# A four-layer kernel of window attention and a 2-D Fourier filter: rows of the filter kept on chip for two groups, and nine smaller moves of work between queues and engines

## The chip, the cores and the metric

The kernel runs on one core of one Trainium2 chip. A core has five engines with instruction streams of their own: TensorE (PE in the profile; matmuls, with weight loads shown as PEld), VectorE (DVE), ScalarE (ACT), GpSimd (POOL) and SyncE (SP, which only issues DMAs here). ScalarE and GpSimd issue DMAs too. TensorE's results go to PSUM, eight banks of 128 partitions x 512 fp32; everything else lives in SBUF or in DRAM. The metric is the time of one execution on the device in microseconds, the median of several runs.

## What is computed

The reference applies two kinds of layer in turn, A, B, A, B, to one sequence of S = 2048 rows with D = 576 columns, all in fp32:

```python
def _A_ref(x, wqkv, wo):
    B, S, D = x.shape
    H = 32; Dh = D // H; W = 256
    qkv = (x @ wqkv).reshape(B, S, 3, H, Dh).transpose(2, 0, 3, 1, 4)
    q, k, v = qkv[0], qkv[1], qkv[2]
    scores = jnp.einsum("bhqd,bhkd->bhqk", q, k) * (Dh ** -0.5)
    idx = jnp.arange(S)
    mask = (idx[:, None] - idx[None, :] >= 0) & (idx[:, None] - idx[None, :] < W)
    p = softmax(where(mask, scores, -1e9))
    o = jnp.einsum("bhqk,bhkd->bhqd", p, v)
    return o.transpose(0, 2, 1, 3).reshape(B, S, D) @ wo

def _B_ref(x, w_r, w_i):
    X = jnp.fft.rfft2(x, axes=(-2, -1)) * (w_r + 1j * w_i)
    return jnp.fft.irfft2(X, s=(S, D), axes=(-2, -1))

x = A_x
for _ in range(2):
    x = x + _A_ref(layernorm(x), A_wqkv, A_wo)
    x = x + _B_ref(layernorm(x), B_w_r, B_w_i)
```

## The kernel before

**Order.** Nothing is scheduled by a planner: every engine executes its instructions in the order in which the Python code writes them, and the framework adds a semaphore wait wherever data or a buffer demands it. So a line moved in the code is an instruction moved within its engine's queue, and an instruction that waits holds up all that stands behind it on that engine. A DMA stands in the queue of the engine that issues it. `layer_a` is written for layers 1 and 3 and `layer_b` for layers 2 and 4; the text calls the first A and first B together layer 1 and the second pair layer 2 (`first` is true in the first `layer_b`, `second` in the second `layer_a`).

**Precision.** Many operands are split into a high part (rounded to fp32r, for a faster matmul) and a low part (the rest). `split_w` (L661) does this for the query/key weights: ScalarE copies the high part (`wqh`, L662), and the engine that it is given subtracts the low part (`wql`, L663). `tail_split` and `tails` do the like for the columns left over behind four blocks of 128.

**Layer A.** The sequence is cut into 16 tiles of 128 rows, the heads into 8 groups of 4. The projections `proj` (L1085; nine weight blocks of 128 columns, four stretches of 512 rows each) feed queries and keys through DRAM. Weight blocks are loaded (`w_load`) and split (`w_split`) while the block before them is in use; block 2 is split while block 1 is projected, in the opening of the attention, where GpSimd also has the memsets of L1232 and L1233. For each tile and head, `score_max` (L1142, L1144) makes the scores and takes the masked maximum, `m_rows` sends the maxima back into the query tile (`qs<-mt`), `exps` (L1179, L1180) makes the scores less the maximum and exponentiates them on ScalarE, GpSimd zeroes what lies outside the window (L1182, L1185), and `part` (L1199) sums the weighted values in the one PSUM bank `U`. After each fourth tile ScalarE copies `U` to `us` (L1204). `norm` (L1210) later transposes these sums (`tpo`, L1213), copies them (`ts`, L1215), divides, and stores the heads' outputs to DRAM. `turned` picks the PSUM bank for `tpo`: a bank of the tag "E" or "S" (three of each) early on, and the single bank "pj" at the end.

The loop `bursts` runs this for tiles 0 to 117 in steps of three heads; with each step it takes at most one or two entries (`tasks`) of the list `due`, which holds the pending `norm` and `m_rows` calls, `norm` sorted last. A drain loop (`for t in range(MIX, NX + 2)`, MIX = 118, NX = 128) writes the last ten tiles out. From tile 120 on `behind` prepares the output projection, the class `Out`, beside it: `out.tail` (GpSimd splits the tail of a tile of attention output), `out.turn` (four transposes into `tpa`, L748 to L751, a cast to `oroom`, L753, by the engine given, a subtraction on VectorE, L757), and loads.

**Output projection and the first filter stage.** `unit` makes 128 rows of the output projection (`ops`, L773) and adds the residual; `ahead(u + 2)` turns the tile two further on (`tpo5p`, `tpo6p` are the first PSUM bank of tiles 5 and 6 there, "q" the second); `sums` and `stats` make the normalization. In the second layer `sums` is two squarings on ScalarE, and `norm` there adds `fy`, a scaling on ScalarE and a subtraction on VectorE. The layernorm of layer B and the first transform are fused to this, one tile n2 of 16 after the other. `f3` (`pz`, L295) is the transform along the rows within a tile, and `f4` (L302 to L341) makes its even and odd halves `ye` (128 x 2 x 290): tile by tile ScalarE copies one half (`half`), VectorE adds and subtracts. In the second layer tiles 12 to 14 instead have their subtraction done by GpSimd from a copy of both halves.

**From the first to the second filter stage.** The second stage works on 16 groups g, and group g needs rows 8g to 8g+7 of all 16 tiles. So `f4` stores each tile whole to DRAM (`yd[0]`, L332), and the second stage reads two groups (a pair) back with one 580 KB load (L470). For the first groups this trip would come last, so tiles 0 to 10 are read back early, in place (L341), and from tile FD = 11 on the rows of these groups are sent from `ye` straight into the pair's tile (L327, `ofree<-ye`, 18 KB each). In the first layer this is done for one pair (groups 0, 1), in the second for two (groups 0 to 3). In the second layer tile 13's stores are issued by GpSimd and tile 14's by ScalarE, whose list `send` is called within tile 15's `f4`, behind its copy; the others go by SyncE. 34 matmuls without use (`warm`, L347) keep TensorE running meanwhile.

**The second filter stage.** `pipe(16, ...)` runs per group: `g0` (loads of the pairs), `gw` (weights not yet there, L202, 580 KB for two groups; the first NW pairs are prefetched during the first stage by `pre`), `g1m` (`p`, L482, the transform down the columns, and the products with the filter on VectorE and GpSimd), `g2` (`pq`, L503, back down the columns, and the halves `ze`, stored whole to `yd[1]` (L540)). `ze` has NY buffers, shared with `ye`, and some of the four `eos`. Groups' rows for the first `near` = 3 tiles of the third stage go straight into their tiles `yis` (L510, `ofree<-ze`) from group FG = 11 on, blocks of earlier groups are read back at groups 10 and 13 (L531). Residuals of two tiles at a time are loaded by `ld` into the pair tiles (`xs`), at groups 11 and 13. 36 more `warm` matmuls end this stage in layer 2.

**The third filter stage.** Per tile n2: `ly` reads the tile (for n2 >= 3), `i1` (`pi`, L566) transforms within the tile and adds the residual, `i2` transposes, `i3` (`po`, L257) makes the output rows. In the first layer the second layer A's opening is fused to it.

## Time and profile before

| | |
|---|---|
| runs | 1384.25, 1384.37, 1386.03 us; median 1384.37 us |
| profiled execution | 1387.98 us, of which the span is 1386.2 us |
| TensorE busy | 1344.4 us (97%), mean granted clock 0.993 |
| VectorE busy | 893.2 us (64%) |
| ScalarE busy | 784.9 us (57%) |
| GpSimd busy | 644.5 us (46%) |
| DMA | 259.12 MB, mean 187 GB/s |

The span begins with the first and ends with the last recorded event of one profiled execution; the time of that execution has 1.8 us around it. Busy time is the sum of an engine's own instructions, without waits and without issuing DMAs. "PE p L482 <- DMA ofree<-ye: 7.3, 1, 7.3" in a list of waits says that the matmuls of line 482 that write `p` waited for a DMA from `ye` into `ofree` (the big tile which holds the pair tiles), 7.3 us in all, once, at the longest 7.3. A row of a timeline gives the start in us, the duration, the engine, line, operation, output<-inputs with shapes, and in brackets the idle time of the engine before it and what ended it; `SPq` and `ACTq` are the queues of SyncE and ScalarE at their DMA issues. A row of the stretches has, behind the window: the span of the core that falls in it; the busy time of PE, PEld, and then of DVE, ACT and POOL, each with its number of instructions; the granted TensorE clock as a share of full speed; the share of time in which the DMA engines were busy; and GB/s.

### The profile page before, as it was taken

How to read it: one execution, taken by the hardware profiler on the slowest of the kernel's cores; microseconds unless marked ns; L12 is line 12 of the kernel's file. 1: busy time of each engine (PE TensorE's matmuls, PEld its weight loads, DVE VectorE, ACT ScalarE, POOL GpSimd, SP SyncE). 2: the span in 40 equal slices, each digit the busy share in tenths (PEclk: the TensorE clock that was granted, in tenths of full speed). 3: DMA queues.
4: the chain of work that ended last, by engine and by line, in shares of the span. 5: the costliest groups of instructions: out<-in, count | busy, mean ns of one | idle time of the engine just before them, and what ended most of it. 6: DMA issues, size and time to landing. Idle time of an engine off the chain costs nothing.

```text
span 1386.2 us, 33596 instructions
## 1 busy us (share of the span) xinstructions
PE 1344.4 (97%) x11356; PEld 1001.6 (72%) x11356; DVE 893.2 (64%) x3046; ACT 784.9 (57%) x1978; POOL 644.5 (46%) x1152
## 2 busy tenths in 40 slices
PE   9999999999999999999999999999999999997998
PEld 8985656666665699975999965566666655996588
DVE  5417777777778266666663157777778774574855
ACT  5622767777778544542455316677777778463223
POOL 2257545555546533476221394455455458111821
PEclk9999999999999999999999999999999999999999
DMA  6756655655446447678763467565554564597874
GB/s 200 209 165 187 192 181 163 187 170 165 149 143 183 123 146 250 221 233 272 262 217 73 127 189 219 158 175 166 159 157 138 160 173 134 154 380 225 275 235 160
DMA packets 202480, 259.12 MB, mean 187 GB/s; under 512 B 104589, under 2 KB 109965, under 8 KB 201797
## 3 DMA queue, kind: packets, MB, share of 16 engines
q1 hardware_dynamic: 191573, 235.70, 56.2%
q10 hardware_dynamic: 7856, 15.33, 3.2%
q0 software_dynamic: 2880, 5.93, 1.7%
q8 instruction: 92, 1.51, 0.5%
q14 instruction: 79, 0.65, 0.1%
HBM read 155.98 MB, written 101.01 MB: 185 GB/s over the span
## 4 chain that ended last, share of the span: by engine, by line
PE 81%; DMA 5%; ACT 4%; POOL 3%; DVE 3%; issue 2%; SPq 1%; ACTq 0%; DVEq 0%; POOLq 0%
PE pj L1085 17%; PE S L1142 12%; PE U L1199 11%; PE vps L978 8%; PE ops L773 7%; PE E L1179 5%; PE po L257 4%; PE pf L257 2%; PE p L482 2%; PE pi L566 2%; PE pq L503 2%; PE tpo L1213 2%; ACT P L1180 2%; DMA qs<-mt 2%; PE pz L295 2%
## 5 line engine op out<-in xcount | busy, mean ns | idle before, releaser
L1144 DVE CUSTOM_DVE_ANT_0 jk<-S,mask 128x384 bf16<-128x384 f32 (+2 forms) x1024 | 491.0, 528 | 120.1 <-PE E L1179 58.8
L1180 ACT ACTIVATE P<-E 128x384 f32<-128x384 f32 (+2 forms) x1024 | 409.8, 477 | 129.8 <-PE E L1179 101.6
L1182 POOL TENSOR_SCALAR_AFFINE_SELECT P<-P 128x512 f32<-128x512 f32 x256 | 162.5, 635 | 288.1 <-ACT P L1180 264.2
L1142 PE MATMUL S<-ks,qs 63*128 63x384 f32 (+2 forms) x1024 | 269.7, 373 | 0.6 <-DVE m L1144 0.4
L1179 PE MATMUL E<-qs,ks 64*128 64x384 f32 (+2 forms) x1024 | 224.0, 373 | 7.3 <-DMA qs<-mt 5.0
L1142 PEld LDWEIGHTS S<-ks,qs 63*128 63x128 f32 x1024 | 141.0, 186 | 105.3 <-DVE m L1144 72.8
L1199 PE MATMUL U<-P,vq 128*19 128x128 f32 (+1 forms) x3840 | 188.4, 329 | 0.9 <-ACT us L1204 0.9
L1085 PE MATMUL pj<-xh,wqh 128*128 128x512 f32 x360 | 157.6, 438 | 1.3 <-DVE sg L1100 0.8
L1199 PEld LDWEIGHTS U<-P,vq 128*19 128x19 f32 x3840 | 96.0, 99 | 78.0 <-issue 23.0
L1185 POOL TENSOR_SCALAR_AFFINE_SELECT P<-P 128x512 f32<-128x512 f32 x224 | 142.1, 634 | 0.0
L1179 PEld LDWEIGHTS E<-qs,ks 64*128 64x128 f32 x1024 | 114.7, 186 | 23.0 <-ACT P L1180 10.4
L1085 PE MATMUL pj<-xh,wql 128*128 128x512 f32 x360 | 125.0, 420 | 2.7 <-POOL wql L663 2.7
L1085 PE MATMUL pj<-xl,wqh 128*128 128x512 f32 x288 | 123.1, 427 | 0.0
L773 PE MATMUL ops<-oroom 128*128 128x290 f32 (+1 forms) x812 | 115.3, 298 | 0.2
L773 PEld LDWEIGHTS ops<-oroom 128*128 128x128 f32 x812 | 110.3, 189 | 0.7 <-DVE ofree L796 0.7
L1085 PEld LDWEIGHTS pj<-xh,wqh 128*128 128x128 f32 x360 | 68.4, 190 | 32.4 <-issue 11.0
L1100 DVE TENSOR_TENSOR sg<-pj,sg 128x512 fp32r<-128x512 f32 x72 | 49.5, 687 | 56.1 <-ACT sg L1097 56.1
L1144 DVE DVE_READ_ACCUMULATOR2_ANT m<- 128x1 f32 x1024 | 84.8, 83 | 0.0
L1097 ACT CAST sg<-pj 128x512 fp32r<-128x512 f32 x72 | 42.2, 586 | 73.3 <-PE pj L1085 58.0
L1085 PEld LDWEIGHTS pj<-xh,wql 128*128 128x128 f32 x360 | 64.4, 189 | 23.5 <-issue 10.7
L978 PE MATMUL vps<-wvh,xh 128*128 128x288 f32 x320 | 71.5, 305 | 0.0
L1085 PEld LDWEIGHTS pj<-xl,wqh 128*128 128x128 f32 x288 | 54.9, 190 | 18.2 <-issue 11.4
(596 smaller groups left out, 2260.7 us busy)
## 6 DMA issues: line engine op xcount, KB each, us to landing
qk_d<-sg SPq DMA_DIRECT2D x56, 512.0 KB
qs<-qk_d SPq DMA_DIRECT2D x384, 72.0 KB
ks<-qk_d SPq DMA_DIRECT2D x348, 72.0 KB
v_d<-vt SPq DMA_DIRECT2D x32, 304.0 KB
vq<-v_d SPq DMA_DIRECT2D x16, 608.0 KB
wt<-in_w SPq DMA_DIRECT2D x16, 580.0 KB
ofree<-x SPq DMA_DIRECT2D x16, 580.0 KB
x<-ofree SPq DMA_DIRECT2D x32, 290.0 KB
```

The source lines that it names most:

```text
L257: T.matmul(ps[:, c, 0:NF], tail[r] if si == 4 else hl_(si), dcs[b // 2][r, b % 2], start=mi == si == 0, stop=si == 4)
L773: self.nc.tensor.matmul(self.ps[u][n][:, 0:self.n], x, self.w[p][:, (2 * wk + n) * self.n:(2 * wk + n + 1) * self.n], start=first and i == ...
L978: T.matmul(ps[:, n, 0:288], xT(xk, c), w[:, wk, n * 288:(n + 1) * 288], start=i == 0, stop=i == len(ks) - 1)
L1085: T.matmul(box["ps"].rearrange("r (n p) -> r n p", n=NT) if second else box["ps"], w[:, wk], x, start=s == 0, stop=s == len(ks) - 1)
L1100: V.tensor_sub(rest[:, 1], by, rest[:, 0].bitcast(F32))
L1142: T.matmul(ps[:, 0:N], q[b:b + 63, pair, i * 128:i * 128 + 128], k[b:b + 63, pair, lo:hi], start=True, stop=True)
L1144: V.tensor_tensor_reduce(out=jk[:, 0:N], in0=ps[:, 0:N], in1=mask[:, 384 - N:384], scale=1.0, scalar=-3e38, op0=ALU.add, op1=ALU.max, accu ...
L1179: T.matmul(ps[:, 0:nq], k[b:b + 64, pair, j * 128:j * 128 + 128], q[b:b + 64, pair, j * 128:j * 128 + nq], start=True, stop=True)
L1180: A.activation(p[:, hl_, 0:nq], ps[:, 0:nq], AF.Exp, scale=SC)
L1182: P.affine_select(out=p[:, :, 0:128], in_=p[:, :, 0:128], pattern=[[0, 4], [1, 128]], compare_op=ALU.is_ge, fill=0.0, base=0, channel_mult ...
L1185: P.affine_select(out=p[:, :, 256:384], in_=p[:, :, 256:384], pattern=[[0, 4], [-1, 128]], compare_op=ALU.is_gt, fill=0.0, base=0, channel ...
L1199: T.matmul(U[32 * h:32 * h + 19, (q0 % 4) * 128:(q0 % 4) * 128 + 128 * (q1 - q0)], vts[n][:, j, h], pt[n, j][:, h, (q0 - j) * 128:(q1 - j) ...
```

## The change

- **Rows (second layer's `f4`).** Rows are sent straight for groups 0 and 1 alone, with one in-place load; `ye` has five buffers. Tile 12 goes by SyncE as before, with two rows less. Tiles 13, 14 and 15 are held and all sent within tile 15's `f4`, behind its two VectorE instructions, in this order: tile 13's two rows (GpSimd), tile 14's first (SyncE) and second (GpSimd), tile 15's two (SyncE), then whole tile 13 (GpSimd), whole 15 (SyncE), whole 14 (GpSimd). GpSimd thus has done all three of its subtractions before it issues any of them, and ScalarE issues none. In the second layer the pair of groups 2 and 3 is read back from DRAM like the others, in two halves.
- **Filter weights.** NW is 5 in both layers: the sixth pair of weights in the second layer is loaded in the second stage.
- **Residual load behind the last stores.** `ld(0)` stays at group 11; `ld(2)` moves from group 13 to the end of group 15, behind the last stores.
- **Rows of groups 13 and 14 for the second tile** go by GpSimd at group 14.
- **Tile 3's load first.** `ly` issues tile 3's load at n2 = 0 and the later ones as before.
- **Tile 2's sums (second layer).** `sums(2)` and `norm(2)` move from ahead of the loop to behind `unit(3)` and `ahead(5)`.
- **Weight 2's low part** is subtracted by VectorE; the other blocks stay with GpSimd.
- **Last sums and transposes.** For the last twelve tiles `us` is copied by VectorE; in the drain `ts` is copied by VectorE, and `tpo` of blocks c > 1 takes a bank of tag "S". The last step of `bursts` takes no tasks, and `due` is sorted once more before the drain.
- **Tails** of tiles 0 to 2 are split one query tile earlier in the drain; tile 3's is split at the same place as before.

```diff
@@ -144,7 +144,7 @@
     yd = [dram.tile([16, 16, 8, 2 * NF], F32, name=f"yd{j}") for j in range(2)]
     OPEN = *range(2, 17, 2), 17
     FD, FG, SH = 11, 11, 192
-    near, NY = 3, 3 if first else 4
+    near, NY = 3, 3 if first else 5
...
@@ -203,7 +203,7 @@
...
-        NW = 5 if first else 6
+        NW = 5
 
         def pre(n2):
 
@@ -310,35 +310,42 @@
             else:
                 both = ip.tile([128, 2, NF], F32, tag="both", name=f"half{n2}", bufs=2)
                 A.copy(both[:, 0], pz[:, 1, 0:NF])
-                if not first and n2 == NT - 1:
-                    hs[n2 - 1]["send"]()
                 V.tensor_add(ye[:, 0], pz[:, 0, 0:NF], both[:, 0])
                 V.tensor_sub(ye[:, 1], pz[:, 0, 0:NF], both[:, 0])
             yef = ye.rearrange("p j f -> p (j f)")
             pre(n2)
-            wide = 1 if first else 2
             if n2 == FD:
-                for k in range(wide):
-                    y_tile(k)
-            eng = nc.sync if n2 < NT - 3 or n2 == NT - 1 else P if first is (n2 == NT - 2) else nc.sync if first else nc.scalar
-
-            def rows(lo, hi):
-                for g in range(lo, hi):
-                    eng.dma_start(ys[g][8 * n2:8 * n2 + 8].rearrange("p c f -> p (c f)"), yef[8 * g:8 * g + 8])
-
-            def send():
-                if n2 >= FD:
-                    rows(0, 2 if n2 == NT - 1 else 2 * wide)
+                y_tile(0)
+
+            def row(eng, g):
+                eng.dma_start(ys[g][8 * n2:8 * n2 + 8].rearrange("p c f -> p (c f)"), yef[8 * g:8 * g + 8])
+
+            def whole(eng):
                 eng.dma_start(yd[0][:, n2], yef)
-                if n2 == NT - 1:
-                    rows(2, 2 * wide)
-            if eng is nc.scalar:
-                h["send"] = send
+
+            if n2 < FD:
+                whole(nc.sync)
+            elif first or n2 < NT - 3:
+                e = P if n2 == NT - 2 else nc.sync
+                for g in range(2):
+                    row(e, g)
+                whole(e)
             else:
-                send()
+                h["rows"] = [lambda e, g=g: row(e, g) for g in range(2)]
+                h["whole"] = whole
+            if not first and n2 == NT - 1:
+                a, b, c = hs[n2 - 2:]
+                a["rows"][0](P)
+                a["rows"][1](P)
+                b["rows"][0](nc.sync)
+                b["rows"][1](P)
+                c["rows"][0](nc.sync)
+                c["rows"][1](nc.sync)
+                a["whole"](P)
+                c["whole"](nc.sync)
+                b["whole"](P)
             if n2 == FD:
-                for k in range(wide):
-                    nc.sync.dma_start(pairs[k].rearrange("p (a f) -> p a f", a=2)[0:8 * FD], yd[0][2 * k:2 * k + 2, 0:FD].rearrange("a n i f -> (n i) a f"))
+                nc.sync.dma_start(pairs[0].rearrange("p (a f) -> p a f", a=2)[0:8 * FD], yd[0][0:2, 0:FD].rearrange("a n i f -> (n i) a f"))
 
         def warm(n):
 
@@ -436,13 +443,15 @@
                 if u > 5:
                     out.load_o(u)
                 out.tail(u)
-            for u in (1, 2):
-                out.sums(u)
-                norm(u)
+            out.sums(1)
+            norm(1)
             for u in range(3, NT - 1):
                 out.load_x(u + 2)
                 out.unit(u, pp)
                 out.ahead(u + 2, pp, False)
+                if u == 3:
+                    out.sums(2)
+                    norm(2)
                 if u + 5 < NT:
                     out.load_o(u + 5)
                     out.tail(u + 5)
@@ -466,7 +475,7 @@
         def g0(g, h):
             if g % 2 == 0 and g not in ys:
                 y = y_tile(g // 2).rearrange("p a c f -> p a (c f)")
-                for a in ((0, 1), (1, 2)) if g == (2 if first else 4) else ((0, 2),):
+                for a in ((0, 1), (1, 2)) if g == 2 else ((0, 2),):
                     nc.sync.dma_start(y[:, a[0]:a[1]], yd[0][g + a[0]:g + a[1]].rearrange("a n i f -> (n i) a f"))
             h["y"] = ys[g]
 
@@ -482,8 +491,8 @@
                     T.matmul(ps[64 * j:64 * j + 64, c, 0:NF], fc[:, g, j, c], h["y"][:, j], start=True, stop=g > 0)
                     if g == 0:
                         T.matmul(ps[64 * j:64 * j + 64, c, 0:NF], fc[:, 16, j, c], h["y"][:, 1 - j], start=False, stop=True)
-            if g in (11, 13):
-                ld(g - 11)
+            if g == 11:
+                ld(0)
             w = wt[g]
             p1 = tws[g % 2]
             p2 = wp.tile([128, 2, NF], F32, tag="tc", name=f"p2_{g}", bufs=3)
@@ -530,11 +539,13 @@
                 for n2 in range(near):
                     nc.sync.dma_start(yis[n2][8 * lo:8 * hi].rearrange("p c f -> p (c f)"), yd[1][n2, lo:hi].rearrange("g i f -> (g i) f"))
             if g == 14:
+                rows(P, 1, 13)
+                rows(P, 1, 14)
                 for k in range(FG, 14):
                     rows(P, 2, k)
             if FG <= g < 15:
-                for n2 in range(2):
-                    rows(P if g == 14 and n2 else nc.sync, n2, g)
+                for n2 in range(1 if g > 12 else 2):
+                    rows(nc.sync, n2, g)
 
             def store():
                 (P if g == 14 else nc.scalar if g < 13 and (g < 8 or g % 2 == 0) else nc.sync).dma_start(yd[1][:, g], yef)
@@ -542,6 +553,8 @@
                 held.append(store)
             else:
                 store()
+            if g == 15:
+                ld(2)
 
         zs, held = {}, []
         pipe(16, [(10, g2), (7, g1m), (2, gw), (0, g0)])
@@ -555,9 +568,9 @@
             next(nxt)
 
         def ly(n2, h):
-            y = h["y"] = yis[n2 % 4]
-            if n2 >= near:
-                nc.sync.dma_start(y.rearrange("p c f -> p (c f)"), yd[1][n2].rearrange("g i f -> (g i) f"))
+            h["y"] = yis[n2 % 4]
+            for k in (near,) if n2 == 0 else (n2,) if n2 > near else ():
+                nc.sync.dma_start(yis[k % 4].rearrange("p c f -> p (c f)"), yd[1][k].rearrange("g i f -> (g i) f"))
 
         def i1(n2, h):
             pi = pp.tile([128, 2, 512], F32, tag="mm", name=f"pi{n2}", bufs=3)
@@ -873,7 +886,7 @@
             h = bp.tile([128, 5, 128], F32R, tag="wqh", name=f"wqh{i}", bufs=2)
             l = bp.tile([128, 5, 128], F32R, tag="wql", name=f"wql{i}", bufs=2)
             wt[i] = (h, l)
-            split_w(nc, raw, h, l, P)
+            split_w(nc, raw, h, l, V if i == 2 else P)
             if i + 2 < 9:
                 w_load(i + 2)
 
@@ -1201,18 +1214,18 @@
                                  start=j == max(e - 1, 0), stop=j == i or (i == e and j == i - 2), skip_group_check=True)
                 if half and i % 4 == 3:
                     us[n, i // 4] = u = wp.tile([128, 512], F32, tag="us", name=f"us{n}_{i}", bufs=1)
-                    A.copy(u, U)
+                    (V.tensor_copy if x >= MIX - 2 else A.copy)(u, U)
 
             def pv(x):
                 part(x, 0)
                 part(x, 1)
 
-            def norm(n, c):
-                tp = turned(f"tpo{n}_{c}")
+            def norm(n, c, drain=False):
+                tp = pp.tile([128, 4, 128], F32, tag="S", name=f"tpo{n}_{c}", bufs=3) if drain and c > 1 else turned(f"tpo{n}_{c}")
                 for a in range(4):
                     T.transpose(tp[:, a], us[n, c][:, a * 128:a * 128 + 128], ident)
                 ts = wp.tile([128, 16, 19], F32, tag="ts", name=f"ts{n}_{c}", bufs=1)
-                A.copy(ts, tp.rearrange("p a (h e) -> p (a h) e", e=32)[:, :, 0:19])
+                (V.tensor_copy if drain else A.copy)(ts, tp.rearrange("p a (h e) -> p (a h) e", e=32)[:, :, 0:19])
                 rc = wp.tile([128, 16, 1], F32, tag="rc", name=f"rc{n}_{c}", bufs=2)
                 V.reciprocal(rc, ts[:, :, 18:19])
                 o = wp.tile([128, 4, 72], F32, tag="o", name=f"o{n}_{c}", bufs=2)
@@ -1317,7 +1330,7 @@
                             new.append((norm, *divmod(x // 4, 4)))
 
                     due.sort(key=lambda z: z[0] is norm)
-                    tasks = [] if took and not spread else due[:1 + (len(due) > 2)]
+                    tasks = [] if took and not spread or 3 * k + 3 >= len(es) else due[:1 + (len(due) > 2)]
                     del due[:len(tasks)]
                     n = 0
                     if k in unit and k not in values:
@@ -1377,8 +1390,8 @@
                 if t == NX - 1:
                     out.last(slice(64, 96), slice(0, 128))
 
-                if t - OB - 4 in (0, 1, 2, 4):
-                    out.tail(min(t - OB - 4, 3))
+                if t - OB - 3 in (0, 1, 2, 5):
+                    out.tail(min(t - OB - 3, 3))
                 if t - OB - 5 in (0, 1, 2):
                     u = t - OB - 5
                     out.turn(u, pp.tile([128, 512], F32, tag="pj", name=f"tpa{u}", bufs=1), V)
@@ -1395,6 +1408,7 @@
             for f in bursts():
                 f()
                 done += 1
+            due.sort(key=lambda z: z[0] is norm)
             for t in range(MIX, NX + 2):
                 loads(t)
                 for pair in range(2):
@@ -1408,7 +1422,7 @@
                 if MIX < y < NX - 1 and y % 4 == 3 and t != NX - 1:
                     due.append((norm, *divmod(y // 4, 4)))
                 for f, *a in due[:1]:
-                    f(*a)
+                    f(*a, *([True] if f is norm else []))
                     due.pop(0)
                 behind(t)
             assert not due
```

## The prediction

> **What bounds the kernel now.** I read the page's head and its chain first, then the list of who TensorE waited for, then the clock in the stretches after the longest waits, and last the timelines of the places that the diff touches.
>
> ```profile
> span 1386.2 us, 33596 instructions
> ...
> PE 81%; DMA 5%; ACT 4%; POOL 3%; DVE 3%; issue 2%; SPq 1%; ACTq 0%; DVEq 0%; POOLq 0%
> ```
>
> Four fifths of the chain is TensorE itself, and no edit removes TensorE work. So the change can only earn the waits of TensorE, and what follows from them. The list of these waits, over the whole span (line, releaser: total us, times, longest):
>
> ```profile
> PE p L482 <- DMA ofree<-ye: 7.3, 1, 7.3
> ...
> PE pi L566 <- DMA ofree<-ze: 4.0, 2, 2.8
> PE pj L1085 <- POOL wql L663: 2.7, 2, 1.8
> ...
> PE tpo L1213 <- ACT us L1204: 1.4, 2, 0.7
> ...
> PE tpa L748 <- ACT ts L1215: 1.1, 2, 0.6
> ...
> PE tpo6p L748 <- DVE oroom L757: 0.9, 1, 0.9
> PE U L1199 <- ACT us L1204: 0.9, 2, 0.5
> ```
>
> Each of these rows is a place that the diff edits; together they are 18.3 us. A wait costs more than itself, as the granted clock (third number from the right) shows in the stretches behind four of them:
>
> ```profile
> 108.00:112.00 4.00, 3.07 (x11) 1.75 (x11) 0.33 (x3) 0.58 (x1) 3.90 (x5) 0.74 0.52 150
> 112.00:116.00 4.00, 4.00 (x18) 2.86 (x17) 3.47 (x14) 0.00 (x0) 3.93 (x5) 0.83 0.47 150
> 812.00:816.00 4.00, 3.11 (x16) 1.84 (x15) 1.79 (x9) 0.59 (x1) 3.90 (x4) 1.00 0.62 192
> ...
> 1277.00:1281.00 4.00, 3.76 (x18) 2.26 (x20) 0.00 (x0) 0.00 (x0) 0.00 (x0) 0.54 0.54 131
> ...
> 652.00:656.00 4.00, 3.94 (x11) 2.97 (x12) 1.77 (x4) 0.86 (x2) 0.69 (x3) 0.58 0.94 295
> ```
>
> Behind the waits of 1.8, 7.3 and 2.8 us the clock is down for some 4 us; behind the one of 0.9 us (812:816) it is not. The loss is 4 x (0.26 + 0.17) = 1.7 us, 4 x 0.46 = 1.8 us and 4 x 0.42 = 1.7 us of matmul time.
> The Trainium skill ("TensorE: Matmul & The Clock Gate", Part 1) has the clock halved only after an idle window of about 3.4 us, free-running; by it the waits of 1.8 and 2.8 us would as a rule cost no clock, and the sum below would be about 1.0 us smaller. The two rows above speak against it here.
>
> **The change part by part.**
>
> **Weight 2's low part on VectorE (both layers).** In layer 1:
>
> ```profile
> 99.48 0.73 ACT L662 CAST wqh<-wqr 128x640 fp32r<-128x640 f32 x1 [1.16 <-DVE sg L1100]
> ...
> 101.53 0.69 DVE L1100 TENSOR_TENSOR sg<-pj,sg 128x512 fp32r<-128x512 f32 x1 [2.48 <-ACT sg L1097]
> ...
> 107.35 1.53 POOL L663 TENSOR_TENSOR wql<-wqr,wqh 128x640 fp32r<-128x640 f32 x1
> ```
>
> The high part is there at 100.2, but GpSimd comes to the low part only at 107.35, behind its queue of memsets. VectorE is idle for 2.48 us before 101.53. The same subtraction costs it 0.69 x 640/512 = 0.86 us (ends: 0.69 of the smaller tile, 1.53 of GpSimd), done by about 101.1, hidden there, six us before TensorE needs it. If that cover were gone the cost would be 0.86 us. GpSimd's later memsets come 1.5 us earlier as well. Gain in layer 1: 1.8 of wait plus 1.0 to 1.7 of clock; I take 2.8 (0.5 if the next DMA waits of the attention opening take it back). In layer 2: 2.7 - 1.8 = 0.9 and no clock (0.3 to 1.0).
>
> **Last sums and transposes by VectorE, tails one tile earlier (both layers).**
>
> ```profile
> 454.00:460.00 6.00, 5.50 (x74) 2.90 (x67) 0.00 (x0) 6.00 (x17) 5.27 (x8) 1.00 0.43 115
> ```
>
> ```profile
> L1204 ACT COPY us<-U 128x512 f32<-128x512 f32 x4 | 2.4, 590 | 0.5 <-PE U L1199 0.5
> ...
> L1215 ACT COPY ts<-tpo 128x304 f32<-128x304 f32 x3 | 1.3, 446 | 0.5 <-PE tpo L1213 0.4
> ```
>
> ```profile
> L753 DVE CAST oroom<-tpa 128x512 fp32r<-128x512 f32 x3 | 2.1, 691 | 5.0 <-PE tpa L749 5.0
> ```
>
> At the end of the attention ScalarE is full (6.00 of 6 us) and VectorE empty. Three of the four copies of the sums and the three of the transposes leave ScalarE: 3 x 0.59 + 1.3 = 3.1 us by their durations, of which those in the full stretch, some 1.5 us, count. VectorE's price is 0.69 (the cast of the same shape) and 0.69 x 304/512 = 0.41, in idle time. The waits behind these copies (1.4, 1.1 and 0.9 over both layers) go: the first because the last task before the drain is put off, the second because the block in question takes another bank. Copy time and waits overlap, and TensorE at 5.50 of 6 is next in line, as is GpSimd. I take 1.6 us a layer, 3.2 in all (0.6 to 2.4 a layer). The earlier tails add a wait for their loads on GpSimd, with its mask selections behind it; a load late by 1 us would cost 1 us.
>
> **Sums of tile 2 behind unit 3 (layer 2).**
>
> ```profile
> 1199.04 0.27 PE L749 MATMUL tpo5p<-ident,ofree 128*128 128x128 f32 x1
> ...
> 1202.67 0.56 ACT L753 CAST oroom<-tpo5p 128x512 fp32r<-128x512 f32 x1
> ```
>
> Tile 5 is transposed at 1199.3, but ScalarE copies it only at 1202.67, after the squares and the scaling of tile 2; TensorE then waits 0.9 us for the same bank. Put behind the copy, these are first needed one unit later. Gain 0.9 (0 to 1.0).
>
> **Rows to two groups, GpSimd subtracting ahead (layer 2, first to second filter stage).**
>
> ```profile
> 1264.60 0.81 POOL L309 TENSOR_TENSOR ye<-half 128x290 f32<-128x290 f32 x1 [1.15 <-ACT half L299]
> ...
> 1265.27 4.71 PE L347 MATMUL warm<-dc 128*128 128x290 f32 x34
> 1265.34 8.50 SPq L327 DMA_DIRECT2D ofree<-ye  x4
> ...
> 1266.33 0.45 DVE L316 TENSOR_TENSOR ye<-pz,half 128x290 f32<-128x290 f32 x1
> ...
> 1269.20 2.78 ACTq L327 DMA_DIRECT2D ofree<-ye  x4
> ```
>
> ```profile
> SPq L327 <- DMA ofree<-ye: 5.9, 1, 5.9
> ```
>
> ```profile
> 1269.20 2.65 DMA ofree<-ye
> ...
> 1274.57 2.43 DMA ofree<-ye
> ...
> 1283.06 2.15 PE pq L503 x8
> ```
>
> ```profile
> yd<-ye POOLq DMA_DIRECT2D x1, 290.0 KB, 3.8
> ...
> ofree<-ye POOLq DMA_DIRECT2D x4, 18.1 KB, 4.5
> ```
>
> SyncE issues one row of tile 12 at 1265.34 and then stands for 5.9 us, until the row that ScalarE issued for tile 14 at 1269.20 has landed. No data ties the two; I read it as the order in which the two queues' completion semaphores were dealt out, an inference. Tile 15's rows, ready at 1266.8, go out behind it at 1274.57. The change takes ScalarE out of these stores, so nothing holds SyncE but data. Issues: SyncE had 3 x 5 and two in-place loads, and gets 3 + 3 + 1 + 3 and one; ScalarE 5 and then none; GpSimd 5 both times, now behind its third subtraction. With 0.65 us an issue SyncE sends tile 12 by 1266, tile 14's first row at 1266.1, tile 15's rows at 1266.8 and 1267.5 and its whole store at 1268.2. GpSimd subtracts from 1264.6 to 1266.0 and, at 0.52 an issue (2.09 for four in that stretch), sends its last store at 1268.2. Landings at 2.65 (SyncE) to 4.5 (GpSimd): group 0 is there at about 1270.5, just after the warm-up matmuls end at 1269.98, group 1 at 1271.5, so the wait of 7.3 and the 1.8 of clock go. The fifth ye buffer lets tiles 13 to 15 lie unsent without a wait.
> Late next is pair 1 (groups 2 and 3), which is now read back from memory after the last whole store: 1268.2 + 3.8 = 1272.0, then a load of 290 KB at 2.65 to 4.32 (this size, third stage below; I take 3.5): 1275.6. Group 2's matmuls then end at 1276.6, and the first pq follows, against 1283.06. Gain 6.5 (ends 3.0 and 8.0). The sixth pair of weights, 580 KB, moves from tile 11 to the second stage; layer 1 runs with five prefetched already.
>
> **Residual load behind the last stores, tile 3's load first (both layers, second to third stage).**
>
> ```profile
> 1317.16 5.08 PE L347 MATMUL warm<-dc 128*128 128x290 f32 x36
> ...
> 1320.12 1.30 SPq L510 DMA_DIRECT2D ofree<-ze  x2
> ```
>
> ```profile
> 648.72 1.57 SPq L510 DMA_DIRECT2D ofree<-ze  x2
> ```
>
> ```profile
> 1326.56 4.32 DMA ofree<-yd
> ```
>
> The waits of 4.0 us (2.8 in layer 1, 1.2 in layer 2) hang on group 15's rows, issued last on SyncE. One row moves to GpSimd, so they leave 0.65 us earlier; the 580 KB load in front of the block reads goes too. GpSimd's own rows for tile 2 come one issue, 0.5 us, later, for a tile that is used third. Gain in layer 2: 0.65 to 1.2 of wait and up to 0.4 at tile 3; I take 1.1. In layer 1: 0.65 to 2.0, clock not counted (1.7 if the wait falls under about 1 us); I take 1.0. SyncE now stands at tile 3's load until group 15's store has landed; behind it are the residuals of tiles 4 to 7, needed rounds later. If tile 2's residual came late, VectorE would stall by as much (loss up to 1).
>
> **Sum:** 2.8 + 0.9 + 3.2 + 0.9 + 6.5 + 1.0 + 1.1 = 16.4 us. The profiled execution took 1387.98 (span 1386.2 and 1.8 around it) and becomes 1371.6. It lies 3.6 above the median of the runs, 1384.37, which becomes 1368.0.
>
> **The rivals.**
> **(B)** The 5.9 us are a backlog of transfers, not an order. Then the rows leave early but land after 4.5, stores too, and pair 1 after 4.32: 1268.8 + 4.5 + 4.3 + 1.0 gives the first pq at 1278.6, less 1.5 of clock: gain 3.0 there, 12.9 in all, 1371.5. Against it: the row issued at 1269.20 landed in 2.65. The Trainium skill ("Trainium Kernel Development and Optimization", Key Constraints) speaks for it: DMAs from SyncE, ScalarE and GpSimd share 16 DMA engines, and another issuing engine saves issue time alone.
> **(C)** The waits of the attention and of tile 2 are only handed on: to the loads of scaled maxima in the opening, to TensorE and GpSimd at its end. Then the filter layers' 6.5 + 1.0 + 1.1 remain: 1375.8. For it: TensorE at 5.50 of 6 in the stretch 454:460.
> **(D)** It does not do what it says: C, and the hold in the rows stays between SyncE and GpSimd. Then the last whole store goes at 1274.57 + 2 x 0.65 = 1275.9 and pair 1 makes the first pq 1275.9 + 3.8 + 3.5 + 1.0 = 1284.2, a loss of 1.1 against 1.0 + 1.1 won: 1383.4.
> **(E)** Slower: in layer 2's second filter stage the weights' sixth pair and pair 1's whole load, 1.2 MB more, hold up ScalarE's eleven stores, and the PSUM copies queued behind each, for which the second matmuls' banks wait. From 16.4 / 11 = 1.5 us a store the gain is gone; at 2.2 us it is 24.2 - 16.4 = 7.8 slower, 1392. Against it: layer 1 runs the same stage with this very setting.
>
> **How the numbers follow.** Forecast 62%, B 15%, C 13%, D 4%, E 6%. Forecast, B and C are all faster: 90%; D within 0.2% (2.8 us, about what runs of this kernel can tell): 4%; E 6%. The terms' low ends (0.5, 0.3, 1.2, 0, 3.0, 0.65, 0.65) give 6.3, their high ends 3.5, 1.0, 4.8, 1.0, 8.0, 3.7, 1.6 give 23.6; they will not all fall together, so 1362 to 1377, which takes in B and C.
>
> **What would show it.** Right: no wait of SyncE over 1 us in the rows, the first p within 1 us of the last warm-up matmul, the first pq some 7 us after it instead of 13; no wait on wql, and a clock of 1.00 at 108:116; no row for tpo6p. Wrong: p of group 2 waiting over 4 us for its load; ScalarE still 6.00 of 6 at the attention's end; a new wait in the second stage.

## The result, and the profile after

| | before | after |
|---|---|---|
| runs, median (lowest to highest) | 1383.68 us (1379.62 to 1386.03, 6 runs) | 1372.28 us (1370.11 to 1375.64, 6 runs) |
| profiled execution | 1387.98 us | 1370.11 us |
| TensorE busy | 1344.4 us | 1337.2 us |

The ratio is 0.9923, 95% interval 0.9902 to 0.9944: 10.7 us, between 7.7 and 13.6 (the two medians alone would give 11.4). Measured again beside three of the experiments, the changed kernel took 0.9892 (0.9872 to 0.9912) of the time before: 15.0 us. The two intervals overlap; taken together they leave 8 to 18 us. The forecast was 1368.0 in a range of 1362 to 1377, a gain of 16.4. The two profiled executions lie 17.9 us apart, more than the runs: the one before was slow among its kind, the one after the fastest of six. So single stretches are compared below, not whole spans.

The head and the chain of waits in the page of the changed kernel:

```profile
span 1368.4 us, 33594 instructions
...
PE 87%; DMA 4%; DVE 3%; ACT 2%; issue 2%; POOL 1%; SPq 0%; ACTq 0%; DVEq 0%; POOLq 0%
```

TensorE's share of the chain rose from 81% to 87%. Its list of waits after (the lines from L482 on now stand 9 to 13 further down):

```profile
PE p L491 <- DMA ofree<-yd: 3.2, 1, 3.2
PE wo L257 <- DVE et L251: 3.1, 1, 3.1
PE E L1192 <- DMA qs<-mt: 2.5, 2, 2.0
...
PE tp0q L245 <- POOL tl L236: 1.7, 1, 1.7
...
PE pi L579 <- DMA ofree<-ze: 0.4, 1, 0.4
```

The waits on wql and ts, at tpo6p, and those on us at `tpo` and `U` are gone, and those at pi for rows are down from 4.0 to 0.4. But three rows of 8.0 us in all are new (of `tp0q` all but 0.3): group 2's `p` waits for the second pair's read-back, and in the places where `pi` waited, `wo` (layer 1) and `tp0q` (layer 2) now wait. The change from the first to the second filter stage, in the timeline of the changed kernel:

```profile
1252.72 4.81 PE L354 MATMUL warm<-dc 128*128 128x290 f32 x34
...
1255.04 1.10 POOL L324 DMA_DIRECT2D yd<-ye x2
1255.63 0.58 SPq L324 DMA_DIRECT2D yd<-ye  x1
...
1257.46 0.71 PE L491 MATMUL p<-ofree,fc 128*64 128x290 f32 x4
...
1260.76 2.37 SPq L479 DMA_DIRECT2D ofree<-yd  x5
...
1263.89 1.20 PE L491 MATMUL p<-ofree,fc 128*64 128x290 f32 x8 [3.23 <-DMA ofree<-yd]
...
1265.02 2.22 PE L512 MATMUL pq<-uv,m 128*128 128x290 f32 x8
```

The first `p` follows the warm-up matmuls without a gap, where it waited 7.3 us before. The three whole stores go out between 1255.0 and 1256.2, yet SyncE can issue the read-back only at 1260.76, when the last of them has landed, 5 us later. The first `pq` comes 12.3 us after the first warm-up matmul, against 17.8 (1283.06 less 1265.27) before. SyncE's waits there (1250 to 1266):

```profile
SPq L479 <- DMA yd<-ye: 4.3, 1, 4.3
...
SPq L321 <- DVE ye L308: 1.3, 1, 1.3
```

At its rows (L321) SyncE now waits for data alone; the 1.3 us for VectorE's half of a tile are a little over the 1 us that the forecast had named as the limit.

Where the time went is measured on stretches of TensorE's own sequence, which the edits leave nearly alike. Each stretch runs from the start of one of its matmuls to that of another (counted in the order of their starts). The last two columns are means over the profiles that lack a part and that have it (their number in brackets), of all the kernels in this study but those that change the stretch otherwise.

| stretch | before | after | without the part | with it |
|---|---|---|---|---|
| layer 1's opening, matmul 640 to 1300 (wql) | 96.3 | 89.9 | 93.5 (5) | 90.3 (9) |
| layer 2's opening, 6500 to 6900 (wql) | 59.7 | 59.8 | 60.4 (5) | 60.0 (9) |
| layer 1's attention end, 3900 to 4190 | 27.47 | 25.26 | 27.47 (5) | 25.25 (9) |
| layer 2's attention end, 9600 to 10060 | 46.97 | 42.89 | 45.6 (5) | 43.2 (9) |
| layer 2, 10150 to 10300 (sums of tile 2) | 20.81 | 20.33 | 20.8 (5) | 20.2 (9) |
| layer 2's first to second warm-up matmuls (rows) | 51.9 | 46.5 | 53.1 (4) | 48.2 (4) |
| layer 1's second filter stage to layer 2's opening, 5100 to 6500 (stores, loads) | 212.4 | 212.1 | 211.6 (6) | 212.3 (6) |
| layer 2's second warm-up matmuls to the end of the last matmul (stores, loads) | 64.4 | 64.4 | 64.7 (6) | 64.5 (6) |

Single profiles spread about some of these means: layer 1's opening took 91.6 to 96.3 us without the part and 89.3 to 91.7 with it, the stretch between the warm-ups 51.9 to 54.6 and 46.5 to 49.7.

### The profile page after: what moved, and what is told of

Same layout as the page of the kernel before. It is cut to its first block, busy times and chain, and to the rows that moved or that the text cites. A ratio compares the mean times of both kernels' runs of the same rounds, so it can differ in the third digit from the quotient of the medians.

```text
span 1368.4 us, 33594 instructions
## 1 busy us (share of the span) xinstructions
PE 1337.2 (98%) x11356; PEld 998.4 (73%) x11356; DVE 901.1 (66%) x3060; ACT 780.3 (57%) x1966; POOL 644.1 (47%) x1152
## 4 chain that ended last, share of the span: by engine, by line
PE 87%; DMA 4%; DVE 3%; ACT 2%; issue 2%; POOL 1%; SPq 0%; ACTq 0%; DVEq 0%; POOLq 0%
PE pj L1098 18%; PE S L1155 12%; PE U L1212 12%; PE vps L991 8%; PE ops L786 7%; PE E L1192 6%; PE po L257 4%; PE pq L512 3%; PE p L491 2%; PE tpo L1226 2%; PE pf L257 2%; PE pi L579 2%; PE pz L295 2%; DMA qs<-mt 1%; PE tpm L1168 1%
## 5 line engine op out<-in xcount | busy, mean ns | idle before, releaser
L1192 PEld LDWEIGHTS E<-qs,ks 64*128 64x128 f32 x1024 | 113.6, 185 | 20.2 <-ACT P L1193 9.3
L1098 PEld LDWEIGHTS pj<-xh,wql 128*128 128x128 f32 x360 | 64.3, 189 | 20.3 <-issue 10.7
L1098 PEld LDWEIGHTS pj<-xl,wqh 128*128 128x128 f32 x288 | 54.5, 189 | 18.2 <-issue 11.4
```

The source lines that it names most:

```text
L1098: T.matmul(box["ps"].rearrange("r (n p) -> r n p", n=NT) if second else box["ps"], w[:, wk], x, start=s == 0, stop=s == len(ks) - 1)
L1192: T.matmul(ps[:, 0:nq], k[b:b + 64, pair, j * 128:j * 128 + 128], q[b:b + 64, pair, j * 128:j * 128 + nq], start=True, stop=True)
```

## The experiments

**The four parts one by one.** Each is the kernel before with one part of the diff.

```diff
 rows_only
-    near, NY = 3, 3 if first else 4
+    near, NY = 3, 3 if first else 5
-        NW = 5 if first else 6
+        NW = 5
...
 wql_only
-            split_w(nc, raw, h, l, P)
+            split_w(nc, raw, h, l, V if i == 2 else P)
 attn_end_only
-                    A.copy(u, U)
+                    (V.tensor_copy if x >= MIX - 2 else A.copy)(u, U)
...
 filter_order_only
+            if g == 15:
+                ld(2)
...
```

(The lines left out are those of the same part in the diff above: of the rows all of `f4` and `g0`; of the attention end also `norm`, `tasks`, `due` and the tails; of the filter order `sums(2)`, the two `rows(P, 1, ...)` and `ly`.)

> Kernel before with the rows edit alone (two groups, GpSimd subtracting ahead, fifth ye buffer, five weight pairs). Theory (the hold of SyncE behind ScalarE's row goes, and the second pair's read-back is the next wait): as in the trace of the changed kernel, the first p within 1 us of the last warm-up matmul, a wait of 3 us on the second pair's load, the stretch some 5.4 us shorter, and the time 4 to 6.5 us below before (ratio 0.9953 to 0.9971). Rival 1 (transfers are backed up, the queues' order was not the cause): a wait of 5 us or more at the first p, gain under 3 us. Rival 2 (the second filter stage pays for the sixth weight pair): new waits on wt or on pq's copies, gain under 3 us although the first p is early.

> Kernel before with weight 2's low part on VectorE alone. Theory: both waits on wql go and with the first of them one clock window of 3.4 us at half speed; 3.4 us in layer 1's opening, 0.4 to 0.9 in layer 2's, 3.3 to 4.3 in all (ratio 0.9969 to 0.9976). Rival (the opening hands it on): the waits on the scaled maxima (qs<-mt) in the same layer grow by as much and less than 1.5 us are left of it at the end of layer 1's attention.

> Kernel before with the end of the attention alone (us and ts by VectorE, tpo in another bank, tails one tile earlier, no task in the last burst). Theory: the waits on us and ts go and ScalarE has free time there; 2.2 us a layer, 4.4 in all (ratio 0.9968), as the trace of the changed kernel has between the last part of the attention and the output projection. Rival (TensorE or GpSimd takes the place of ScalarE): under 1 us a layer.

> Kernel before with tile 2's sums, the later residual load, tile 3's early load and the two rows on GpSimd alone. Theory (GpSimd's own rows now land last and the tiles of the third stage, which lie on the memory that they are read from, wait for them): 1.0 us from the sums, nothing at either entry to the third stage; in layer 1 a wait of about 3 us at wo, in layer 2 one of 1.7 at tp0q, in place of those at pi; 0 to 1.5 us below before in all. Rival (what the prediction had): both waits at pi shrink with nothing in their place, 2.1 us more.

| kernel | ratio, 95% interval | us won | forecast |
|---|---|---|---|
| rows_only | 0.9961 (0.9947 to 0.9976) | 5.4 | 6.5 |
| wql_only | 0.9972 (0.9960 to 0.9985) | 3.9 | 3.7 |
| attn_end_only | 0.9968 (0.9954 to 0.9983) | 4.4 | 3.2 |
| filter_order_only | 0.9999 (0.9988 to 1.0011) | 0.1 | 3.0 |

The parts add up to 13.8 us. This lies within the second measurement of the whole and 0.2 us above the interval of the first (7.7 to 13.6), which is less than any part's own interval leaves open. The fourth part, tile 2's sums, the two moved loads and the two rows on GpSimd, brought nothing. TensorE's waits in that kernel:

```profile
PE wo L257 <- DVE et L251: 3.3, 1, 3.3
...
PE pi L572 <- DMA ofree<-yd: 1.3, 1, 1.3
```

The wait at `wo` is there by this part alone. The one expected at `tp0q` is not: in layer 2 TensorE waited at `pi`, 1.3 us for a load and 0.9 for a copy of ScalarE's. In wql_only TensorE waited 0.2 us for the scaled maxima in all, against 5.0 before, so the opening did not hand the gain on. (This wait varies between profiles, up to 3.6 us in the last kernel below, which has the part too; what speaks against the rival is the time, 3.9 us.)

**Who held SyncE.** The kernel before, with only the engine of tile 14's stores changed:

```diff
-            eng = nc.sync if n2 < NT - 3 or n2 == NT - 1 else P if first is (n2 == NT - 2) else nc.sync if first else nc.scalar
+            eng = nc.sync if n2 < NT - 3 or n2 == NT - 1 else P if not first or n2 == NT - 2 else nc.sync
...
-                if not first and n2 == NT - 1:
-                    hs[n2 - 1]["send"]()
```

> Kernel before with tile 14's stores issued by GpSimd in place of ScalarE, and nothing else: still four groups of rows, as many bytes. Theory (the order of the two queues held SyncE): no wait of SyncE at its rows over 1 us, the wait at the first p falls from 7.3 to 8.8 us to under 4. Rival (a backlog of transfers): SyncE still stands 4 us or more at its second row of tile 12 and the wait at the first p stays over 6 us.

It took 0.9943 (0.9924 to 0.9962), 7.9 us less than before, with the same rows, bytes and buffers. SyncE's list of waits from 1245 to 1275, and TensorE's from 1255, in this kernel:

```profile
...
SPq L325 <- DMA ofree<-yd: 2.3, 2, 1.6
...
```

```profile
PE p L480 <- DMA ofree<-ye: 3.4, 1, 3.4
```

The wait of 5.9 us behind a row is gone from SyncE's list. (Of the theory's numbers one did not hold: a wait of 1.6 us on earlier read-backs is left in the rows.) The first `pq` comes 12.3 us after the first warm-up matmul, as in the changed kernel. The stretch between the warm-ups took 46.8 us, where the four kernels with the whole rows edit took 46.5 to 49.7: the rest of that edit (two groups for four, held stores, the fifth buffer) is not shown to earn anything beyond this line.

The trace of before shows the link that the prediction inferred. SyncE's second row of tile 12 and ScalarE's first row of tile 14 signal their end on one semaphore, number 102; ScalarE's row has landed at 1271.85, and SyncE goes on at 1271.86. ScalarE was late in its turn, because that row needs GpSimd's third subtraction, which stood behind five DMA issues of GpSimd's own:

```profile
1265.81 2.09 POOL L327 DMA_DIRECT2D ofree<-ye  x4 [0.40 <-DVE ye L308]
...
1268.46 0.71 POOL L309 TENSOR_TENSOR ye<-half 128x290 f32<-128x290 f32 x1
1269.20 2.78 ACTq L327 DMA_DIRECT2D ofree<-ye  x4
```

In the traces of before, of the changed kernel and of the second of the next two kernels, SyncE and ScalarE use the same eight semaphores (101 to 109 without 106) for the ends of their DMAs, GpSimd eight others. Two more kernels put ScalarE back among these stores. One sends rows for four groups again, those of groups 2 and 3 by ScalarE:

```diff
+                z["rows"][2](nc.scalar)
                 b["rows"][0](nc.sync)
+                z["rows"][3](nc.scalar)
                 b["rows"][1](P)
+                a["rows"][2](nc.scalar)
...
```

> The changed kernel with rows again sent straight for four groups, those of groups 2 and 3 by ScalarE, which is idle there. Theory (the wait of 3.2 us at the second pair is its trip through DRAM behind three whole stores): the wait at group 2's p goes, none over 1 us takes its place, 2 to 3.5 us below the changed kernel. Rival (the third pair, read back behind the same stores, is late instead): a wait of 1.5 us or more at group 4's p, under 1.5 us won. Rival 2 (rows from ScalarE hold up SyncE again): a wait of SyncE over 2 us at its rows and no gain.

The other has ScalarE send the whole stores of tiles 13 and 14:

```diff
-                a["whole"](P)
+                a["whole"](nc.scalar)
+                b["whole"](nc.scalar)
                 c["whole"](nc.sync)
-                b["whole"](P)
```

> The changed kernel with the whole stores of tiles 13 and 14 issued by ScalarE, which is idle there from 1253.4 us on, in place of GpSimd behind its rows. Theory (the second pair waits for the last of three whole stores, and these queue behind the rows): ScalarE's two stores are issued some 1.5 us earlier and landed before SyncE's; the wait at group 2's p falls from 3.2 to 3.5 us to about 2, 1 to 1.5 us below the changed kernel. Rival 1 (the bytes set it: 870 KB of stores at the rate of the 16 engines): the wait stays over 3 us. Rival 2 (ScalarE's stores hold SyncE's last store or loads back by the order of the queues): SyncE waits 2 us or more at its rows or at whole 15, and the time is 1 us or more above.

Of SyncE's waits, in the first (1243 to 1262) and in the second (1245 to 1275), those at its rows and stores for other queues' rows and stores:

```profile
SPq L323 <- DMA ofree<-ye: 4.3, 1, 4.3
```

```profile
SPq L324 <- DMA yd<-ye: 1.8, 1, 1.8
SPq L321 <- DMA yd<-ye: 1.5, 1, 1.5
```

Both holds are back, for rows in the one and for stores in the other, each for what ScalarE sends there; no data ties SyncE's rows and stores to them. In the second the trace names the link again: ScalarE's store of tile 14 and SyncE's store of tile 15 signal their end on one and the same semaphore, 108, and SyncE's issue at 1255.02 waits until ScalarE's store, issued at 1249.75, has landed at 1255.00. So here the hold comes of a transfer that lasted 5.3 us, not of a late issue. The first took 0.9905 (0.9891 to 0.9920), with 6.7 us of wait at the first `p`; the second 0.9894 (0.9878 to 0.9909), with 1.2 us at the first and 3.5 us at group 2's `p`. Neither gained on the changed kernel. In the second each wait is under the 2 us that rival 2 had named (3.3 together), and the wait at group 2's `p` stayed over 3 us, as rival 1 had it, so that run does not part the two.

**What the third stage waits for.** The changed kernel with group 14's whole store moved from GpSimd to ScalarE:

```diff
                 A.copy(both[:, 1], pq[:, 1, 0:NF])
+                nc.scalar.dma_start(yd[1][:, 14], zs[14])
...
-                (P if g == 14 else nc.scalar if g < 13 and (g < 8 or g % 2 == 0) else nc.sync).dma_start(yd[1][:, g], yef)
+                (nc.scalar if g < 13 and (g < 8 or g % 2 == 0) else nc.sync).dma_start(yd[1][:, g], yef)
```

> The changed kernel with the whole store of group 14 in the second filter stage issued by ScalarE, behind its copy of group 15, in place of GpSimd; both layers. Theory (GpSimd's last two rows land 4.6 us after their issue, for they stand behind its 290 KB store, and the third stage's tiles lie on the memory they are read from): these rows land some 2.2 us after their issue; the wait at wo in layer 1 falls from 3.1 us to under 1 and that at tp0q in layer 2 from 1.7 to under 0.5; 2 to 4 us below the changed kernel. Rival 1 (the residual's 580 KB load fills the transfer engines, the order of the queue does not matter): rows still 4 us or more, same time. Rival 2 (the store is late instead, and tile 3's load behind it): a new wait at tile 3's pi.

The entry to the third stage in the timeline of the changed kernel, layer 1 and then layer 2:

```profile
644.71 0.59 ACT L249 CAST et<-tp 128x512 fp32r<-128x512 f32 x1 [3.97 <-DMA ofree<-eo]
...
646.41 1.61 PE L257 MATMUL wo<-dc,et 128*128 128x290 f32 x10 [3.06 <-DVE et L251]
...
1302.75 0.50 POOL L519 DMA_DIRECT2D ofree<-eo  x1
...
1307.68 0.24 POOL L234 CAST tl<-ofree 128x66 fp32r<-128x66 f32 x1 [3.94 <-DMA ofree<-eo]
```

`et` and `tl` take nothing from that row; they are tiles of the third stage's pool, on memory from which the second stage's rows are still read (`inner` is closed before `bj` is opened), and they wait for the last read. The DMA issues of GpSimd's last two rows in layer 2, changed kernel and then this one, where the window holds the row before them too (KB each, median us from issue to landing):

```profile
ofree<-eo POOLq DMA_DIRECT2D x1, 18.1 KB, 4.6
ofree<-ze POOLq DMA_DIRECT2D x1, 18.1 KB, 4.6
```

```profile
ofree<-ze POOLq DMA_DIRECT2D x2, 18.1 KB, 2.8
...
ofree<-eo POOLq DMA_DIRECT2D x1, 18.1 KB, 2.8
```

Without the 290 KB store ahead of them the rows land 1.8 us sooner. But the store alone does not make them late: in the kernel before they stand behind the same store and land 3.0 to 3.2 us after their issue. There SyncE's two whole stores go out 2.0 and 2.7 us behind GpSimd's; in the changed kernel the first follows it by 0.2 us. In the repeat of the changed kernel it followed by 1.5 us in layer 1, and the rows took 3.1 and 3.7. What each of the two is worth was not measured apart. TensorE's waits at layer 1's entry (630 to 665) in this kernel:

```profile
PE pi L580 <- DMA ofree<-yd: 2.7, 2, 1.6
PE wo L257 <- ACT et L249: 1.5, 1, 1.5
```

In layer 2 the wait at tp0q falls from 1.7 to 0.3, and 1.8 us at `pi` take its place (1.0 of it for a load, for which the repeat of the changed kernel waits 1.1 as well). The time was 0.9895 (0.9878 to 0.9912), beside 0.9892 for the changed kernel on the same chip. So the theory held for who is late, but not in size: the rows took 2.8 us, not 2.2, and 1.5 us are left at `wo`, not under 1. What was won is lost again, as the second rival had it, though at the loads of tiles 4 and 5 and not of tile 3.

**The whole once more, and three versions.**

> The changed kernel once more, beside the next three on one chip. The four parts measured one by one add up to 13.8 us (5.4 + 3.9 + 4.4 + 0.1). Theory (the parts lie in different stages and add): ratio 0.9900, 0.9885 to 0.9915. Rival (the wins share something, as the waits on the scaled maxima): 0.9925 or more, as in the first measurement.

0.9892, as the theory had it. The first measurement, 0.9923, is left unexplained; the two intervals overlap.

The first two `pq` ahead of group 2's `p` in layer 2:

```diff
+        def g1x(g, h):
+            hp[g] = h
+            if g == 2 and not first:
+                for k in range(2):
+                    g2(k, hp[k])
+            g1m(g, h)
...
-        pipe(16, [(10, g2), (7, g1m), (2, gw), (0, g0)])
+        pipe(16, [(10, g2x), (7, g1x), (2, gw), (0, g0)])
```

> The changed kernel with the second matmuls of groups 0 and 1 (pq) written ahead of group 2's first ones in layer 2, so that TensorE has them to do while the second pair is loaded. Theory: 2 x 0.56 = 1.1 us of work falls into the wait at p, which shows as 2.1 to 2.4 us in place of 3.2 to 3.5; 1 us below the changed kernel, too little to be told from it by the times alone, but shown by the stretch. Rival (group 1's products are late, pq waits itself): the same sum of waits.

TensorE's timeline in it:

```profile
1261.56 3.40 PE L512 MATMUL pq<-uv,m 128*128 128x290 f32 x16 [0.66 <-POOL uv L502]
1264.89 2.17 PE L491 MATMUL p<-ofree,fc 128*64 128x290 f32 x16
1268.45 1.20 PE L491 MATMUL p<-ofree,fc 128*64 128x290 f32 x8 [1.38 <-DMA ofree<-yd]
```

The work moved into the wait was 3.4 us, not the 1.1 that I expected, and group 2's `p` does not wait at all; 0.7 us ahead of `pq` and 1.4 at group 4's `p`, for the third pair, are new. From the first to the second warm-up matmuls it took 45.1 us, where the changed kernel's two profiles have 46.5 and 48.4. The time, 0.9899 (0.9884 to 0.9914), can't be told from the changed kernel's.

The kernel before with tile 14's stores on GpSimd, weight 2's low part, the attention's end and tile 2's sums, and nothing else of the change:

> Kernel before with tile 14's stores issued by GpSimd, and of the change only weight 2's low part, the end of the attention and tile 2's sums: without the rows edit and without the moved residual load, tile 3's early load and the two rows on GpSimd. Theory (what these parts won is the release of SyncE alone, and the moved loads won nothing): ratio 0.9943 x 0.9972 x 0.9968 = 0.9883, 0.0005 for the sums below it, so 0.986 to 0.990, level with the changed kernel's 0.9892 or under it. Rival (the rows edit or the moved loads carry 3 us or more beside): 0.9905 or more.

0.9907 (0.9890 to 0.9924): the interval reaches into the theory's range and the rival's, and holds 0.9923 and 0.9892, so it decides nothing. Its stretch between the warm-ups took 46.2 us.

The last has both the early `pq` and the moved store:

> The changed kernel with both of the edits that shortened their stretches: group 14's whole store by ScalarE, and the first two pq ahead of group 2's p in layer 2. Theory: 1.3 us from the second; from the first, waits shift to tile 3's and later loads, so 0 to 1.5 us: 1.3 to 2.8 us below the changed kernel (ratios of it so far 0.9923 and 0.9892), 0.987 to 0.989. Rival (neither is a gain in the time of runs): 0.9892 or more.

1367.54 us median, 0.9885 (0.9856 to 0.9915). Its stretch between the warm-ups was the shortest of all, 44.6 us, but the interval holds the changed kernel's ratios too: no version here is shown to be faster than it.

## Why the prediction came out as it did

**Weight 2's low part: right in size.** 3.9 us alone against 3.7. The mechanism held too: in the changed kernel VectorE subtracts the part in 0.82 us from 100.43 on, where 0.86 and an end at 101.1 were forecast, and the rival that the opening would hand it on fell. But its clock term was a chance, not a price. Two windows of the stretch with the wait on wql, in the kernel before and in rows_only, which has the same wait:

```profile
106.50:109.92 3.42, 1.59 (x9) 1.03 (x6) 1.47 (x8) 0.00 (x0) 3.28 (x4) 1.00 0.70 219
109.92:113.33 3.41, 3.41 (x10) 2.01 (x10) 1.60 (x7) 0.58 (x1) 3.33 (x4) 0.50 0.59 184
```

```profile
106.52:109.94 3.42, 1.64 (x8) 1.11 (x8) 0.87 (x6) 0.00 (x0) 3.27 (x4) 1.00 0.54 158
109.94:113.35 3.41, 3.41 (x18) 2.30 (x18) 3.00 (x12) 0.59 (x1) 3.33 (x5) 1.00 0.77 193
```

TensorE was idle for 1.8 us of both first windows; the second went at half speed in the one and at full in the other. Of the five profiles with this wait three lost the window. Three fifths of 1.7 us are the 1.0 that the forecast had added; that it fits is luck, for the loss was taken as sure.

**The attention's end: right, too small.** Forecast 1.6 us a layer; the table of stretches has 2.2 in layer 1 (27.47 to 25.25, within 0.02 in every profile) and about as much in layer 2. One of the signs of being wrong, ScalarE still at 6.00 of 6, all but showed. This is the stretch after that answers to 454:460:

```profile
447.00:453.00 6.00, 5.86 (x82) 3.12 (x80) 1.42 (x3) 5.97 (x17) 5.75 (x9) 1.00 0.20 56
```

ScalarE is as full as before (5.97 of 6). The room that the copies left was filled by the exponentials behind them, and TensorE rose from 5.50 to 5.86. A full engine that sheds work ends sooner, it does not look emptier.

**Tile 2's sums: right, half the size.** The wait of 0.9 at tpo6p is gone; the stretch around it (matmuls 10150 to 10300) fell from 20.81 to 20.33, and to 20.2 on the mean of the profiles with this part, 0.6 where 0.9 was forecast.

**Rows: right in mechanism, 1 to 2 us too large.** Theory and order of events held: the issues came when forecast (the last whole store 2.9 us after the first warm-up matmul in forecast and trace), the first `p` at once, and the pair's read-back as the next wait. The mis-sized term is the landing of the last whole store: 3.8 us were taken from one GpSimd store alone, but three of 290 KB go out within 1.2 us, and SyncE's took 5.0 (issued at 1255.63, landed at 1260.61; the read-back follows at 1260.76). The load took 3.1, for 3.5 (the low end of its range, 2.65, was read from an 18 KB row, not from a load of this size). So `pq` came 12.3 us after the first warm-up matmul for the 11.3 forecast. A backlog, as rival B has it, is likely for the whole stores: the DMA engines were busy for 76 to 80% of the time from 1256 to 1260. No run shows it apart. For the rows it is not the cause, since one changed queue freed SyncE. And the clock, again: rows_only and the repeat of the changed kernel waited 3.4 and 3.5 us there and went at half speed for two windows and one, the first profile waited 3.2 and lost none; hence 49.7, 48.4 and 46.5 us for the stretch.

**Residual load and tile 3's load: wrong.** 1.0 + 1.1 us were forecast, 0.1 us came of the part by its time, sums included, and by the stretches a loss of 0.7 in layer 1 and 0.2 won in layer 2, both within what profiles of one kind differ. The step that failed is "The waits of 4.0 us ... hang on group 15's rows". They did, but not on these alone. This row stands in the trace of before, 0.04 us behind the `pi` whose wait I read:

```profile
652.10 0.58 ACT L249 CAST et<-tp 128x512 fp32r<-128x512 f32 x1 [2.77 <-DMA ofree<-ze]
```

`et` lies on the old memory and had waited for the reads of it until the same moment. GpSimd's last two rows had landed at 651.44 and 651.79, SyncE's last three at 651.62, 651.97 and 652.15. So the two queues ended 0.4 us apart, and the change shortened one of them. In the changed kernel SyncE's last rows did land sooner, at 641.02 and 641.49, but GpSimd's last two only at 644.34 and 645.10, and `et` waited for the first of these. Counted from GpSimd's first row, SyncE's end came 2.1 us earlier and GpSimd's 1.9 us later. Of these 1.9 us the row that was moved to GpSimd, costed at 0.5 us "for a tile that is used third", explains about 0.4; the rest is the longer time from issue to landing that the experiment above looked into. It was the queue's end that counted, not the tile that the row is for.

**The other rivals.** The page that was cited for B (the Trainium skill, "Trainium Kernel Development and Optimization", Key Constraints) has issuing from several engines save issue time alone; here the exchange of the engine for five DMAs was worth 7.9 us, by what no longer waited. (B's own sum starts at 1268.8, 0.6 us behind the last store of the forecast, without a reason given.) C fell for weight 2 and for the attention's end. D fell with the first `p`, which does not wait. E fell too: TensorE's list (down to 0.3 us) has no wait on the filter's weights and none on the second stage's copies.

**The sum.** By the table's last two columns: 3.2 + 0.4 for weight 2, 2.2 + 2.4 for the attention's end, 0.6 for the sums, 4.9 for the rows, -0.7 and 0.2 for the stores and loads, 13.2 in all. Against the 16.4 that is 2.6 less for the stores and loads, 1.6 less for the rows, 0.3 less for the sums, and 1.4 more at the attention's end. The first measurement of the whole, 10.7, lies below the 13.2, the second, 15.0, above.

## What to carry to other kernels

When a DMA issue waits for another queue's transfer and no data ties them, find out which transfer it waits for, and whether that one is issued late or lasts long, and move it to another queue first: here that one line was worth as much as the whole rearrangement around it. When a wait at a change of stage is to be shortened, list everything that is released within a microsecond of it, the tiles that merely lie on reused memory included, for the next of them takes the wait's place. A few microseconds of gain are measured on stretches between fixed matmuls, in several profiles, since the clock alone moves single executions by as much.

## What the runs showed of the hardware

The half-speed stretches of TensorE lie on a grid: in all fourteen profiles each is 3.41 us long or a multiple of it (the last of a profile, cut off by the end, aside), and their starts within one profile differ by multiples of 3.41. The changed kernel's one in layer 1's third stage shows it:

```profile
644.48:647.89 3.41, 1.48 (x11) 1.48 (x12) 2.15 (x5) 0.86 (x2) 0.69 (x4) 1.00 0.69 220
647.89:651.31 3.42, 3.42 (x14) 3.11 (x14) 0.69 (x1) 1.50 (x3) 0.68 (x4) 0.50 1.04 315
```

This is the free-running window of about 3.4 us that the Trainium skill has ("TensorE: Matmul & The Clock Gate", Part 1), which the prediction set aside; on the length the trace agrees with it. On what halves the clock it does not: the window before was idle for 1.9 us of 3.4 here and for 1.8 before wql, not for all of it, and the same idle time cost nothing in rows_only. Laid on that grid, the windows of all fourteen profiles, without the first 15 us and the end, give this: all 25 in which TensorE was busy for less than 39% of the time were followed by one at half speed, none of the 5433 in which it was busy for more than 78%, and 18 of the 84 between. What decides between these bounds stays open. For an estimate it means that a wait of 1.5 to 3.5 us costs itself and, by chance, 1.7 us more for each window lost (rows_only lost two behind its wait of 3.4).
